# A mixer kernel with other homes for the squares and the gates' weights, and with batch 1's scores over the whole TensorE array

## The chip, the cores and the metric

One core of a Trainium2 chip runs the whole program. The metric is device time in microseconds, and the median of several runs is compared. On a core TensorE (PE), VectorE (DVE), ScalarE (ACT), GpSimd (POOL) and SyncE (SP) each work through a queue of their own; SP here issues nearly all of the transfers between memory (HBM) and SBUF.

## The reference

```python
def _attn_ref(q, k, v):            # B, H, S, D = 2, 8, 768, 64
    k_sum = k.reshape(B, H, nb, 32, D).max(axis=3)      # nb = 24 blocks
    v_sum = v.reshape(B, H, nb, 32, D).mean(axis=3)
    scores_l = scale * q @ k.T                          # kept where |i - j| < 16
    scores_s = scale * q @ k_sum.T + log(32)
    a = softmax(concat(masked scores_l, scores_s))
    return a @ concat(v, v_sum)

def _moe_ref(x, mu_k, mu_r, w_k, w_v, w_r):   # x: B, S, 512; w_k 512x1024
    x_prev = x shifted by one position
    xk = mu_k * x + (1 - mu_k) * x_prev
    xr = mu_r * x + (1 - mu_r) * x_prev
    k = maximum(xk @ w_k, 0)
    return sigmoid(xr @ w_r) * ((k * k) @ w_v)

def _moe2_ref(x, w_tok1, w_tok2, w_ch1, w_ch2):
    h = maximum(x.T @ w_tok1, 0) @ w_tok2     # over the 768 positions
    u = x + h.T
    return u + maximum(u @ w_ch1, 0) @ w_ch2  # 512 -> 1536 -> 512

reference = _moe2_ref(_moe_ref(_attn_ref(q, k, v)))
```

The weights arrive as float64, everything else as float32.

## The kernel before, in words

*Attention.* A tile is 128 positions of one batch. For each tile `s_stage` forms the scores of its 8 heads against 24 block keys and 96 neighbouring keys (120 columns, in `kw`), `t_stage` transposes the exponentials, and `v_stage` multiplies them with the values (`pv`). A head has 64 dimensions, and each half of a tile (64 positions) has its own window of keys, so a score is a 64x120 product of 64-deep operands, and four of them stand in the four quarters of the 128x128 array: two heads (parity `e` = 0, 1 on the two halves of the partitions) by two halves of the tile. One bank of PSUM, tag "s", holds the scores of one parity, four heads by both halves. Batch 0 takes one parity per step, batch 1 both, 16 score matmuls per tile in a fixed line (`in_line`). pv is 64x64 with a depth of 120 and uses half of the array. These products are plain float32, and each shows as two records in the trace.

*Everything else* multiplies in three products of a high and a low part (`mm3`, lines 539 to 546, names `xh`/`xl`, `kh`/`kl`, `gh`/`gl`, and pairs of `w`), each one record on PE. A float64 weight is loaded as words, turned into a float32 by ACT (L153) and DVE (L157, L163), and split by ACT (L174) and POOL (L175).

*The MoE stage* goes in chunks of 256 positions. ko = xk·w_k in 256-column matmuls; `k2_tile` squares the result and splits it into `kh`, `kl`; acc = squares·w_v in 512-column matmuls, the square standing in the array and w_v moving (`values`); ro = xr·w_r the same way (`gate_pass`). Behind it come the token MLP (h and ho) and the channel MLP (go or m, then o at L983 and L955).

*Order.* The program emits attention and the MoE stage side by side by a credit of costs (`attention` and `main`), and a list scheduler with priorities (`ahead`) then fixes the order of each engine's queue. From batch 1 on, scores, transposes and pv stand among ko and acc on PE.

*Where things lie.* [...] Pools grow from the left (const, `ybuf`, stage, work, xp, later w2) and from the right (`r1` with the 16 slots of w_k and w_v, `at` for attention, later `r2` with 12 slots). Before the change `kh` and `kl` lie in work, at 70.7 to 78.7 KB, while w_v lies in r1 at 160 to 224 KB; w_r lies in the first four slots of r2, at 112 to 128 KB, while xr's parts lie at 50.7 to 58.7 KB. `ybuf` at 0.75 to 24.75 KB holds the outputs of the MoE stage for all twelve tiles; in the attention stage part of it serves as room for values.

Of the kernel before, what the change touches and what calls it, by code (L numbers as in the profile page):

```python
# [9 lines left out]
F32 = mybir.dt.float32  # L10
F32R = mybir.dt.float32r
# [16 lines left out]
MW = 256  # L28
# [8 lines left out]
GB = 4  # L37
PIN3, PIN4 = 3, 3
PINL = True
QB = 3  # L40
RSPLIT = 1
HM = 300
VDMA, VEARLY = (1,), 1
# [11 lines left out]


@with_exitstack
def fused_kernel(ctx, tc, q, k, v, vt, mu, w_k, w_v, w_r, w_t1, w_t2, w_c1, w_c2, out):
    nc = tc.nc
    B, NT = q.shape[:2]  # L60
    S, DM = v.shape[1] - WINDOW * 2, v.shape[2]
    H, D = 8, 64
    DFF = w_v.shape[0]
# [158 lines left out]
    def in_line(inst):  # L222

        behind(inst, line[-1:])
        line.append(inst)
# [7 lines left out]
    def after(inst):  # L233

        behind(inst, mark[-1:])
# [8 lines left out]
    for f in range(NF):  # L244
        for i, (src, use) in enumerate(((w_k[f], wk.append),
                                        (w_v[f * 128:(f + 1) * 128, :], wv.append))):
            weights.add(wa if 2 * f + i < NRA else wb, src, use)

    work = pool("work", "left")
    xp = pool("xp", "left", reuse_waits="tile")  # L250
    XB = S + 1
# [95 lines left out]
    @ahead(HL)  # L347
    def q_load(b, t):
        if b == 0:
            st_of(b)["qT"][t] = xT[:, :, XB + 1 + 128 * t:XB + 129 + 128 * t]  # L350
        else:
            st_of(b)["qT"][t] = at.tile([128, NP, 128], F32, tag="qT", bufs=QB, name="qT")
        after(nc.sync.dma_start(st_of(b)["qT"][t], q[b, t]))

    @ahead(HS)
    def s_stage(b, t, es):
        st = state[b]
        mask = masks[1 if t == 0 else 2 if t == NT - 1 else 0]
        kw, qT = st["kw"][t], st["qT"][t]
        sps = [bank("s", 2, [128, NP, NC], "sp") for _ in es]  # L360
        line.clear()
        for p in range(NP):
            for half in range(2):
                c0 = half * (WC - NC)
                for sp, e in zip(sps[::-1], es[::-1]):
                    r = slice(64 * e, 64 * e + 64)
                    m = nc.tensor.matmul(sp[64 * half:64 * half + 64, p], qT[r, p, 64 * half:64 * half + 64],  # L367
                                         kw[r, p, c0:c0 + NC], start=True, stop=True)
                    if len(es) > 1:
                        in_line(m)  # L370
        if PINL:
            mark.append(m)
        zs = []
        for sp, e in zip(sps, es):
            mn = at.tile([128, NP], F32, tag="mn", bufs=4, name="mn")
            if b not in LATE:
                den = at.tile([128, NP], F32, tag="den", bufs=4, name="den")
            else:
                if e == 0:
                    st["den"][t] = at.tile([128, 2, NP], F32, tag="dens", bufs=3, name="dens")  # L380
                den = st["den"][t][:, e]
            P = []
            for p in range(NP):
                pe = at.tile([128, NC], F32, tag="pe", bufs=PEB, name="pe")
                low = nc.vector.tensor_tensor_reduce(out=pe, in0=sp[:, p], in1=mask, op0=ALU.add, op1=ALU.min,  # L385
                                                     scale=-1.0 / math.sqrt(D), scalar=3.0e38, accum_out=mn[:, p:p + 1])
                nc.scalar.activation(pe, pe, AF.Exp, bias=mn[:, p:p + 1], scale=-1.0, accum_out=den[:, p:p + 1])  # L387
                P.append(pe)
            lows.append(low)
            zs.append({"u": (b, t, e), "P": P, "den": den})  # L390
        return zs
# [20 lines left out]
    @ahead(HV)  # L412
    def v_stage(zs):
        b, t, _ = zs[0]["u"]
        st = state[b]
        if t not in st["pv"]:
            st["pv"][t] = bank("pv", 1, [128, NP, 128], "pv")
        pv = st["pv"][t]
        line.clear()
        for p in range(NP):  # L420
            for half in range(2):
                for z in zs[::-1]:
                    e = z["u"][2]
                    h = 2 * p + e
                    m = nc.tensor.matmul(pv[64 * e:64 * e + 64, p, 64 * half:64 * half + 64],  # L425
                                         st["vw"][t][half][0][:, h * D:(h + 1) * D],
                                         z["PT"][:, p, 64 * half:64 * half + 64], start=True, stop=True)
                    if len(zs) > 1:
                        in_line(m)
        if zs[-1]["u"][2] == 1:  # L430
            c0 = b * XB + 1 + 128 * t
            if b not in LATE:
                nc.scalar.copy(xT[:, :, c0:c0 + 128], pv)
            else:
                den = st["den"].pop(t)
                nc.vector.tensor_scalar(den, den, 1e-9, None, ALU.add)
                nc.vector.reciprocal(den, den)
                rb = bank("pt", 2, [128, NP, 128], "rb")
                for p in range(NP):
                    for e in range(2):  # L440
                        nc.tensor.matmul(rb[64 * e:64 * e + 64, p], den[:, e, p:p + 1].to_broadcast([128, D]), ident,
                                         start=True, stop=True)
                x = xT[:, :, c0:c0 + 128]
                nc.scalar.copy(x, pv)
                nc.vector.tensor_tensor(x, x, rb, ALU.mult)
# [64 lines left out]
            q_load(b, 1)  # L510

    def prep(b):

        for t in range(NT):
            k_max(b, t)
            yield HOLD / (NT + 2)
        for j in range(2):
            vt_sum(b, j)
            yield HOLD / (NT + 2)
        kw_sums(b, 0)  # L520
        v_gather(b)
# [29 lines left out]
    @ahead(HM)  # L551
    def k2_tile(o):
        rl = work.tile([128, 2 * MW], F32, tag="rl", bufs=2, name="rl")
        hi = work.tile([128, 2 * MW], F32R, tag="kh", bufs=2, name="kh")
        lo = work.tile([128, 2 * MW], F32R, tag="kl", bufs=2, name="kl")
        nc.scalar.activation(rl, o, AF.Relu)  # L556
        nc.vector.tensor_tensor(rl, rl, rl, ALU.mult)  # L557
        nc.scalar.copy(hi, rl)  # L558
        nc.gpsimd.tensor_tensor(lo, rl, hi.bitcast(F32), ALU.subtract)  # L559
        return hi, lo  # L560
# [81 lines left out]
            q_load(0, t + 1)  # L642
    while weights.todo:
        weights.load()
    masks = []
    for kind in range(3):
        mc = at.tile([128, NC], F32, name=f"mask{kind}")
        mm = work.tile([128, 2, 128], F32, tag="t32", bufs=2, name="mm")
        for half in range(2):
            m = mm[:, half, :NC]  # L650
            nc.gpsimd.memset(m, 0.0)
            first = 64 * half - PAD
            keys = m[:, NB:NC] if half == 0 else m[:, 0:NK]
            for base, cm, st in ((first + EDGE, -1, 1), (EDGE - first, 1, -1)):
                nc.gpsimd.affine_select(out=keys, in_=keys, pattern=[[st, NK]], compare_op=ALU.is_ge, fill=-8.0 * BIG,
                                        base=base, channel_multiplier=cm)
            if kind == 1 and half == 0:
                nc.gpsimd.memset(m[:, NB:NB + PAD], -8.0 * BIG)
            if kind == 2 and half == 1:
                nc.gpsimd.memset(m[:, NK - PAD:NK], -8.0 * BIG)  # L660
            nc.gpsimd.memset(m[:, 0:NB] if half == 0 else m[:, NK:NC], math.sqrt(D) * math.log(BLOCK))
            nc.gpsimd.tensor_scalar(mc[64 * half:64 * half + 64], m[64 * half:64 * half + 64], 1.0, 1.0, ALU.mult, ALU.mult)
        masks.append(mc)
    for t in range(NT):
        ahead(HK)(k_max)(0, t)
    kw_sums(0, 0)
    for z in range(B):
        nc.gpsimd.memset(xT[:, :, z * XB:z * XB + 1], 0.0)
    nc.gpsimd.tensor_scalar(oms, mus, -1.0, 1.0, ALU.mult, ALU.add)
# [20 lines left out]
    R2 = Ring(r2, "w", 12)  # L690
    wr, t1, t2 = [], [], []
    NM = DTOK // 128
    for d in range(KD):
        weights.add(R2, w_r[d * 128:(d + 1) * 128, :], wr.append)
    per = 512 // DTOK
    for i in range(0, NT, per):
        weights.add(R2, w_t1[i * 128:(i + per) * 128, :].rearrange("(a p) n -> p a n", p=128),
# [127 lines left out]
    xp.release()  # L825
    work.release()
    w2 = pool("w2", "left", reuse_waits="tile")
    W2 = Ring(w2, "w", 8)
    CR = Ring(w2, "w", 0)
    CR.slots = R2.slots[:10] + spare + wb.slots + R2.slots[10:]  # L830
    c2_add(0, 0)
    c2_add(0, 1)
    plain_add(2, CR)
# [248 lines left out]
    for got in cd():  # L1082
# [4 lines left out]
                weights.step()  # L1087
    w2.release()
    r2.release()
    r1.release()  # L1090
    stage.release()
    ypool.release()
    const.release()


_INS = ['q', 'k', 'v', 'vt', 'mu', 'moe_w_k', 'moe_w_v', 'moe_w_r',
        'moe2_w_tok1', 'moe2_w_tok2', 'moe2_w_ch1', 'moe2_w_ch2']


def laid_out(q, k, v, mu_k, mu_r, w_k):  # L1100
# [6 lines left out]
    def by_values(x):  # L1107
# [2 lines left out]
    pad = ((0, 0), (0, 0), (WINDOW, WINDOW), (0, 0))  # L1110
    kp = by_values(np.pad(k, pad))
    dm, dff = w_k.shape
    return {
        "q": by_values(q).reshape(B, 2 * D, H // 2, nt, 128).transpose(0, 3, 1, 2, 4),
        "k": np.stack([kp[..., 128 * t:128 * t + 128 + 2 * WINDOW] for t in range(nt)], axis=1),
        "v": np.pad(v, pad).transpose(0, 2, 1, 3).reshape(B, S + 2 * WINDOW, H * D),
        "vt": by_values(v).reshape(B, 2 * D, 2, H // 4 * S).transpose(0, 2, 1, 3),
# [25 lines left out]
```

## Time and profile before

| | |
|---|---|
| median of 3 runs | 503.41 us (502.32 to 503.72) |
| span of the profiled execution | 502.8 us |
| PE busy | 487.9 us, 97% of the span |
| PE's weight loads busy | 407.1 us, 81% |
| DVE, ACT, POOL busy | 316.6, 250.9, 217.4 us |
| granted TensorE clock, mean | 0.990 |

The profile shows no time of the execution beside its span; the median of the runs stands 0.6 us above it. Busy is the union of an engine's instructions, and ends of matmuls are modelled, so the pace of PE is read from one start to the next. A score or pv has two records. [...]

### The profile page before, as it was taken

The numbers are of one execution on the slowest core, as the hardware profiler recorded it, in microseconds if no ns is written. First come the engines' busy times: TensorE is split into PE (matmuls) and PEld (weight loads), VectorE is DVE, ScalarE is ACT, GpSimd is POOL, SyncE is SP. The second block draws the span as 40 slices with busy tenths as digits, with TensorE's granted clock in tenths as the row PEclk, the third lists the DMA queues.
The fourth block names the chain that finished last, engine by engine and source line by source line (L and its number), as shares of the span: only waits on it lengthen the run. The fifth ranks groups of instructions, "written<-read, shape, count | busy, mean of one in ns | idle before, by whom it ended". The sixth has DMA issues, their size and how long they took to land.

```text
span 502.8 us, 8800 instructions
## 1 busy us (share of the span) xinstructions
PE 487.9 (97%) x3278; PEld 407.1 (81%) x3278; DVE 316.6 (63%) x638; ACT 250.9 (50%) x569; POOL 217.4 (43%) x266
## 2 busy tenths in 40 slices
PE   7999997999999999999999998999999999999996
PEld 3567785888888888888888887878898999989995
DVE  2888998641514355598889789646579638354352
ACT  1778746862544555686585455454554435111110
POOL 6335587862441447345516434774942813000000
PEclk9899998899999999999999999999999999999999
DMA  8999930221000650000551998639351405253102
GB/s 264 323 309 361 335 87 14 88 80 40 20 1 2 224 196 0 1 0 14 161 163 21 400 394 313 211 112 316 117 168 42 142 31 164 52 200 117 52 1 83
DMA packets 35914, 70.63 MB, mean 140 GB/s; under 512 B 3072, under 2 KB 12288, under 8 KB 35872
## 3 DMA queue, kind: packets, MB, share of 16 engines
q1 hardware_dynamic: 34288, 69.09, 42.0%
q10 hardware_dynamic: 1584, 0.98, 0.7%
q8 instruction: 26, 0.43, 0.3%
q14 instruction: 16, 0.13, 0.1%
HBM read 60.04 MB, written 9.44 MB: 138 GB/s over the span
## 4 chain that ended last, share of the span: by engine, by line
PE 75%; DMA 10%; DVE 8%; POOL 2%; ACT 2%; issue 1%; SPq 1%; DVEq 0%; POOLq 0%
PE ko L544 13%; PE acc L544 13%; PE o L955 12%; PE m L544 11%; PE o L983 7%; PE ro L544 7%; PE go L544 5%; DMA wst<-in_moe_w_k_dram 3%; DMA xT<-in_q_dram 3%; DMA ybuf<-in_v_dram 2%; DVE wf L163 2%; PE pv L425 2%; PE sp L367 2%; PE h L544 2%; DMA wst<-in_moe_w_ch_dram 1%
## 5 line engine op out<-in xcount | busy, mean ns | idle before, releaser
L175 POOL TENSOR_TENSOR w<-wf,w 128x512 fp32r<-128x512 f32 x50 | 69.1, 1387 | 77.3 <-ACT w L174 72.4
L544 PE MATMUL ko<-xh,w 128*128 128x256 f32 x384 | 76.3, 288 | 1.7 <-POOL w L175 0.9
L544 PE MATMUL m<-u,w 128*128 128x256 f32 x504 | 65.1, 283 | 0.8 <-DVE mw L846 0.7
L544 PEld LDWEIGHTS m<-u,w 128*128 128x128 f32 x504 | 63.4, 191 | 2.9 <-DVE mw L846 0.9
L544 PEld LDWEIGHTS ko<-xh,w 128*128 128x128 f32 x384 | 61.1, 188 | 5.4 <-POOL w L175 1.1
L544 PE MATMUL acc<-w,kh 128*128 128x512 f32 x192 | 61.7, 404 | 0.0
L955 PE MATMUL o<-w,gh 128*128 128x512 f32 x192 | 59.1, 391 | 0.0
L544 PE MATMUL ko<-xl,w 128*128 128x256 f32 x192 | 54.4, 283 | 1.1 <-DVE xl L536 1.1
L559 POOL TENSOR_TENSOR kl<-rl,kh 128x512 fp32r<-128x512 f32 x24 | 33.7, 1405 | 44.6 <-ACT kh L558 36.4
L163 DVE SCALAR_TENSOR_TENSOR wf<-wst,wf 128x512 int32<-128x512 int32 x50 | 47.6, 956 | 8.2 <-ACT wst L153 7.1
L174 ACT CAST w<-wf 128x512 fp32r<-128x512 f32 x50 | 30.9, 620 | 42.8 <-DVE wf L163 40.9
L557 DVE TENSOR_TENSOR rl<-rl 128x512 f32<-128x512 f32 x24 | 19.6, 819 | 48.4 <-ACT rl L556 48.2
L387 ACT ACTIVATE pe<-pe,mn 128x120 f32<-128x120 f32 x96 | 36.6, 383 | 14.6 <-DVE mn L385 14.3
L153 ACT ACTIVATE wst<-wst 128x512 f32<-128x512 f32 x62 | 41.1, 675 | 2.1 <-DMA wst<-in_moe_w_ch_dram 2.1
L544 PEld LDWEIGHTS acc<-w,kh 128*128 128x128 f32 x192 | 35.3, 192 | 7.3 <-ACT pe L387 0.3
L955 PEld LDWEIGHTS o<-w,gh 128*128 128x128 f32 x192 | 34.7, 188 | 6.2
L534 DVE SCALAR_TENSOR_TENSOR xk<-xT,mus,tmp 128x256 f32<-128x256 f32 x52 | 36.5, 733 | 4.1 <-POOL tmp L533 3.2
L544 PEld LDWEIGHTS ko<-xl,w 128*128 128x128 f32 x192 | 36.2, 188 | 2.1 <-DVE xl L536 1.3
L544 PE MATMUL acc<-w,kl 128*128 128x512 f32 x96 | 37.7, 403 | 0.0
L955 PE MATMUL o<-w,gl 128*128 128x512 f32 x96 | 37.1, 391 | 0.0
L544 PE MATMUL go<-u,w 128*128 128x512 f32 x144 | 35.6, 393 | 0.0
L784 ACT ACTIVATE gh<-m 128x512 fp32r<-128x512 f32 x24 | 14.2, 596 | 42.7 <-DVE m L846 42.7
(120 smaller groups left out, 964.5 us busy)
## 6 DMA issues: line engine op xcount, KB each, us to landing
wst<-in_moe_w_ch_dram SPq DMA_DIRECT2D x36, 512.0 KB, 6.9
w<-stored SPq DMA_DIRECT2D x24, 512.0 KB, 4.9
stored<-w SPq DMA_DIRECT2D x24, 256.0 KB, 4.7
wst<-in_moe_w_k_dram SPq DMA_DIRECT2D x8, 512.0 KB, 7.4
wst<-in_moe_w_v_dram SPq DMA_DIRECT2D x8, 512.0 KB, 9.5
wst<-in_moe_w_tok_dram SPq DMA_DIRECT2D x6, 512.0 KB, 4.7
out_dram<-o SPq DMA_DIRECT2D x12, 256.0 KB, 2.4
kw<-in_k_dram SPq DMA_DIRECT2D x9, 320.0 KB, 5.1
```

Source lines behind the costliest of these rows:

```text
L153: a = nc.scalar.activation(top.bitcast(F32), top.bitcast(F32), AF.Prelu, scale=2.0 ** -112, alpha=2.0 ** 32)
L163: nc.vector.scalar_tensor_tensor(wi, top, 3, wi, ALU.logical_shift_left, ALU.bitwise_or)
L174: r = nc.scalar.copy(hi, src)
L175: eng.tensor_tensor(lo, src, hi.bitcast(F32), ALU.subtract)
L387: nc.scalar.activation(pe, pe, AF.Exp, bias=mn[:, p:p + 1], scale=-1.0, accum_out=den[:, p:p + 1])
L534: nc.vector.scalar_tensor_tensor(xk[:, d], xT[:, d, x0:x0 + MW], mu[:, d:d + 1], tmp, ALU.mult, ALU.add)
L544: nc.tensor.matmul(o, l, r, start=(first and i == 0), stop=(last and i == 3 * n - 1))
L557: nc.vector.tensor_tensor(rl, rl, rl, ALU.mult)
L559: nc.gpsimd.tensor_tensor(lo, rl, hi.bitcast(F32), ALU.subtract)
L784: nc.scalar.activation(hi, o, AF.Relu)
L955: nc.tensor.matmul(accs[c][t], l, r, start=(first and j == 0 and i == 0), stop=(last and j == 1 and i == 2))
L983: nc.tensor.matmul(accs[0][t], l, r, start=(k == 0 and i == 0), stop=(k == NF2 - 1 and i == 2))
```

## The change

Three things are edited. First, `kh` and `kl` move from the pool work to a pool `sq` on the right (152 to 160 KB), and w_r moves from r2's slots to a pool `wrp` on the left (28.8 to 44.8 KB), whose four slots later serve as half of the ring `W2`; r2 then lies at 104 to 152 KB and the order of the slots in the ring `CR` changes. Second, batch 1's scores are 8 matmuls of 128x120 per tile: the host lays out q as `qd` with a block of zeros for each head pair, so that a stationary tile of 128x128 holds one half's 64 positions for e = 0 and for e = 1, and a bank now holds one half of the tile for both parities (before: one parity for both halves). The masks for that (`both`) are put together by eight copies on POOL, softmax and v_stage index accordingly, and v_stage issues as many matmuls of the same shape as before. Third, the q tiles of batch 1 are twice as large (512 KB); that of tile 0 has a buffer of its own, and those of tiles 1 to 5 lie in slots of `ybuf` (QHOME). To make room the program's scratch for DMA descriptors shrinks.

```diff
-QB = 3
+QHOME = 8, 10, 6, 8, 10
...
+    sq = pool("sq", "right")
+    wrp = pool("wrp", "left")
...
-            st_of(b)["qT"][t] = at.tile([128, NP, 128], F32, tag="qT", bufs=QB, name="qT")
-        after(nc.sync.dma_start(st_of(b)["qT"][t], q[b, t]))
+            home = slot2(QHOME[t - 1]) if t else at.tile([128, 2 * DM], F32, name="qT")
+            st_of(b)["qT"][t] = home.rearrange("p (g h c) -> p g h c", g=NP, h=2)
+            after(nc.sync.dma_start(st_of(b)["qT"][t], qd[b - 1, t]))
...
-        line.clear()
-        for p in range(NP):
-            for half in range(2):
+        if len(es) == 1:
+            mask = [masks[1 if t == 0 else 2 if t == NT - 1 else 0]]
+            r = slice(64 * es[0], 64 * es[0] + 64)
+            for p in range(NP):
+                for half in range(2):
+                    c0 = half * (WC - NC)
+                    m = nc.tensor.matmul(sps[0][64 * half:64 * half + 64, p], qT[r, p, 64 * half:64 * half + 64],
+                                         kw[r, p, c0:c0 + NC], start=True, stop=True)
+        else:
+
+            mask = [both[:, 1 if t == 0 else 0], both[:, 3 if t == NT - 1 else 2]]
+            line.clear()
+            for half, sp in enumerate(sps):
                 c0 = half * (WC - NC)
-                for sp, e in zip(sps[::-1], es[::-1]):
-                    r = slice(64 * e, 64 * e + 64)
-                    m = nc.tensor.matmul(sp[64 * half:64 * half + 64, p], qT[r, p, 64 * half:64 * half + 64],
-                                         kw[r, p, c0:c0 + NC], start=True, stop=True)
-                    if len(es) > 1:
-                        in_line(m)
+                for p in range(NP):
+                    m = nc.tensor.matmul(sp[:, p], qT[:, p, half], kw[:, p, c0:c0 + NC], start=True, stop=True)
+                    in_line(m)
...
-                for z in zs[::-1]:
-                    e = z["u"][2]
+                for e in (1, 0) if len(zs) > 1 else (zs[0]["u"][2],):
                     h = 2 * p + e
+                    z, c = (zs[half], e) if len(zs) > 1 else (zs[0], half)
                     m = nc.tensor.matmul(pv[64 * e:64 * e + 64, p, 64 * half:64 * half + 64],
                                          st["vw"][t][half][0][:, h * D:(h + 1) * D],
-                                         z["PT"][:, p, 64 * half:64 * half + 64], start=True, stop=True)
+                                         z["PT"][:, p, 64 * c:64 * c + 64], start=True, stop=True)
...
-        hi = work.tile([128, 2 * MW], F32R, tag="kh", bufs=2, name="kh")
-        lo = work.tile([128, 2 * MW], F32R, tag="kl", bufs=2, name="kl")
+        hi = sq.tile([128, 2 * MW], F32R, tag="kh", bufs=2, name="kh")
+        lo = sq.tile([128, 2 * MW], F32R, tag="kl", bufs=2, name="kl")
...
+    both = at.tile([128, 4, NC], F32, name="both")
+    for i, (kind, half) in enumerate(((0, 0), (1, 0), (0, 1), (2, 1))):
+        for e in range(2):
+            rows.append((both[64 * e:64 * e + 64, i], masks[kind][64 * half:64 * half + 64]))
...
+    for dst, src in rows:
+        nc.gpsimd.tensor_copy(dst, src)
...
+    WR = Ring(wrp, "wr", KD)
     for d in range(KD):
-        weights.add(R2, w_r[d * 128:(d + 1) * 128, :], wr.append)
+        weights.add(WR, w_r[d * 128:(d + 1) * 128, :], wr.append)
...
-    W2 = Ring(w2, "w", 8)
+    W2 = Ring(w2, "w", 8 - KD)
+    W2.slots += WR.slots
     CR = Ring(w2, "w", 0)
-    CR.slots = R2.slots[:10] + spare + wb.slots + R2.slots[10:]
+    CR.slots = R2.slots[6:10] + R2.slots[:6] + spare + wb.slots + R2.slots[10:]
```

The change also moves instructions in the queues. In the rows that follow a name such as `acc<-w,kh` is the output and its operands, the shape is that of the output, and xN counts neighbours of one form; the line numbers of after are some ten higher.

First place, PE, where batch 1's tile 3 multiplies with its values. Before, all 16 stand in one block among ko:

```order
L544 MATMUL ko<-xh,w 128x256
L425 MATMUL pv<-PT,vw 64x64 x16
L544 MATMUL ko<-xh,w 128x256
L544 MATMUL ko<-xl,w 128x256
L544 MATMUL ko<-xh,w 128x256
L544 MATMUL acc<-w,kh 128x512 x2
L544 MATMUL acc<-w,kl 128x512
L544 MATMUL acc<-w,kh 128x512 x2
L544 MATMUL acc<-w,kl 128x512
```

Afterwards, two of the 16 come earlier, and the other 14 stand one by one:

```order
L435 MATMUL pv<-PT,vw 64x64
L553 MATMUL ko<-xh,w 128x256
L553 MATMUL acc<-w,kh 128x512
L435 MATMUL pv<-PT,vw 64x64
L553 MATMUL acc<-w,kh 128x512
L435 MATMUL pv<-PT,vw 64x64
L553 MATMUL acc<-w,kl 128x512
L435 MATMUL pv<-PT,vw 64x64
L553 MATMUL acc<-w,kh 128x512
L435 MATMUL pv<-PT,vw 64x64
L553 MATMUL acc<-w,kh 128x512
```

What moved: pv of this tile went from one place between ko to 14 places between ko and acc, mostly after every single acc.

Second place, PE, the scores of batch 1's tiles 0 and 1. Before, they are 64x120 matmuls, 14 and 1 of tile 0 with four acc between, then batch 0's last pv with its reciprocal sums (rb):

```order
L544 MATMUL ko<-xh,w 128x256
L367 MATMUL sp<-kw,qT 64x120 x14
L544 MATMUL acc<-w,kh 128x512 x4
L367 MATMUL sp<-kw,qT 64x120
L425 MATMUL pv<-PT,ybuf 64x64 x8
L441 MATMUL rb<-ident,dens 64x128 x8
L544 MATMUL ko<-xh,w 128x256
```

Afterwards tile 0's 8 stand together, and tile 1's first four come six rows of acc behind the last row shown:

```order
L379 MATMUL sp<-kw,qT 128x120 x8
L553 MATMUL acc<-w,kh 128x512 x4
L553 MATMUL ko<-xh,w 128x256
L553 MATMUL ko<-xl,w 128x256
L320 MATMUL vp<-ident,vrs 24x128 x2
L435 MATMUL pv<-PT,ybuf 64x64 x8
L451 MATMUL rb<-ident,dens 64x128 x8
```

What moved: the odd 64x120 score between acc and batch 0's last pv is gone, two ko and the sums of the values' blocks (vp) stand in its place, and tile 1's scores begin earlier among acc and ko.

Third place, DVE, as batch 1 begins. Before, the conversion of the last weights of the MoE stage (L157 and L163) and the input mix (xk) stand in front of the first softmax row of tile 0 (L385):

```order
L445 TENSOR_TENSOR xT<-xT,rb 128x4x128
L157 TENSOR_SCALAR wf<-wst 128x512
L534 SCALAR_TENSOR_TENSOR xk<-xT,mus,tmp 128x256
L163 SCALAR_TENSOR_TENSOR wf<-wst,wf 128x512
L534 SCALAR_TENSOR_TENSOR xk<-xT,mus,tmp 128x256
L557 TENSOR_TENSOR rl<-rl 128x512
L157 TENSOR_SCALAR wf<-wst 128x512
L385 ISA pe,mn<-sp,mask_182 128x120
```

Afterwards all eight softmax rows of tile 0 stand in front of these (the last one is the first row here, L395), and the first rows of tile 1 (the last row here) come soon behind:

```order
L395 ISA pe,mn<-sp,both 128x120
L395 ISA mn 128x1
L157 TENSOR_SCALAR wf<-wst 128x512
L455 TENSOR_TENSOR xT<-xT,rb 128x4x128
L163 SCALAR_TENSOR_TENSOR wf<-wst,wf 128x512
L157 TENSOR_SCALAR wf<-wst 128x512
L543 SCALAR_TENSOR_TENSOR xk<-xT,mus,tmp 128x256
L406 TENSOR_SCALAR den<-den 128x4
L163 SCALAR_TENSOR_TENSOR wf<-wst,wf 128x512
L543 SCALAR_TENSOR_TENSOR xk<-xT,mus,tmp 128x256
L395 ISA pe,mn<-sp,both 128x120
```

What moved: the softmaxes of tile 0 went ahead of the last conversions and of the mix.

## Rows read from the trace of the kernel before

**Rows 1.** the page's head: the span, and each engine's busy time and instructions.

```profile
span 502.8 us, 8800 instructions
...
PE 487.9 (97%) x3278; PEld 407.1 (81%) x3278; DVE 316.6 (63%) x638; ACT 250.9 (50%) x569; POOL 217.4 (43%) x266
```

**Rows 2.** Two stretches: us, PE busy (xrecords), granted clock, DMA share, GB/s.

```profile
92.00:300.00 208.00, 207.94 (x1418) 1.00 0.30 102
380.00:496.00 116.00, 116.00 (x724) 1.00 0.26 82
```

**Rows 3.** PE's timeline: start us, us, work, xrecords, [idle before <-releaser].

```profile
80.32 0.39 PE L544 MATMUL ko<-xh,w 128*128 128x256 f32 x1 [0.74 <-ACT rl L556]
...
81.75 0.50 PE L544 MATMUL ko<-xh,w 128*128 128x256 f32 x2 [0.93 <-POOL w L175]
...
84.71 0.63 PE L367 MATMUL sp<-kw,qT 64*64 64x120 f32 x2 [1.52 <-issue]
...
307.48 1.89 PE L983 MATMUL o<-w,gh 128*128 128x512 f32 x7 [1.29 <-ACT gh L784]
```

**Rows 4.** PE's timeline, single pv pieces between ko of batch 1's tile 2.

```profile
114.46 1.04 PE L425 MATMUL pv<-PT,vw 120*64 120x64 f32 x28
115.43 0.38 PE L544 MATMUL ko<-xh,w 128*128 128x256 f32 x1
115.74 0.33 PE L425 MATMUL pv<-PT,vw 120*64 120x64 f32 x2
...
116.58 0.50 PE L544 MATMUL ko<-xh,w 128*128 128x256 f32 x2
```

**Rows 5.** the chain that ended last: start us, us, what, xrecords.

```profile
127.34 2.80 PE acc L544 x12
...
151.72 2.84 PE ko L544 x24
...
211.97 4.43 PE ro L544 x19
...
313.26 2.75 PE o L983 x12
```

**Rows 6.** PE's timeline, a block of pv between acc.

```profile
148.89 0.39 PE L544 MATMUL acc<-w,kh 128*128 128x512 f32 x1
149.21 1.15 PE L425 MATMUL pv<-PT,vw 120*64 120x64 f32 x32
150.29 0.50 PE L544 MATMUL acc<-w,kh 128*128 128x512 f32 x1
150.62 0.39 PE L544 MATMUL acc<-w,kl 128*128 128x512 f32 x1
```

**Rows 7.** PE's timeline, two pieces of scores and the ko behind each.

```profile
93.05 1.04 PE L367 MATMUL sp<-kw,qT 64*64 64x120 f32 x30
94.03 0.51 PE L544 MATMUL ko<-xh,w 128*128 128x256 f32 x2
...
130.07 0.64 PE L367 MATMUL sp<-kw,qT 64*64 64x120 f32 x14
130.64 0.39 PE L544 MATMUL ko<-xh,w 128*128 128x256 f32 x1
```

**Rows 8.** PE's groups by shape: xrecords | busy us, mean ns | idle before.

```profile
L544 PE MATMUL acc<-w,kh 128*128 128x512 f32 x192 | 61.7, 404 | 0.0
...
L367 PE MATMUL sp<-kw,qT 64*64 64x120 f32 x192 | 11.7, 299 | 1.6 <-issue 1.5
```

**Rows 9.** PE in two stretches of the start, columns as in rows 2.

```profile
84.00:90.00 6.00, 5.29 (x38) 0.50 0.23 60
90.00:91.00 1.00, 1.00 (x4) 0.62 0.93 291
```

**Rows 10.** POOL's groups by shape: xinstructions | busy us, mean ns | idle before.

```profile
L662 POOL TENSOR_SCALAR mask<-mm 64x120 f32<-64x120 f32 x6 | 1.7, 286 | 0.3
```

**Rows 11.** DMA issues: queue, xcount, KB each, median us to landing.

```profile
qT<-in_q_dram SPq DMA_DIRECT2D x6, 256.0 KB, 3.2
```

More of the change, by code (lines that the diff above doesn't have):

```diff
@@ L57, in fused_kernel @@
 @with_exitstack
-def fused_kernel(ctx, tc, q, k, v, vt, mu, w_k, w_v, w_r, w_t1, w_t2, w_c1, w_c2, out):
+def fused_kernel(ctx, tc, q, qd, k, v, vt, mu, w_k, w_v, w_r, w_t1, w_t2, w_c1, w_c2, out):
     nc = tc.nc
-    B, NT = q.shape[:2]
+    B, NT = k.shape[:2]
     S, DM = v.shape[1] - WINDOW * 2, v.shape[2]
@@ L350, in q_load @@
             st_of(b)["qT"][t] = xT[:, :, XB + 1 + 128 * t:XB + 129 + 128 * t]
+            after(nc.sync.dma_start(st_of(b)["qT"][t], q[t]))
         else:
-            st_of(b)["qT"][t] = at.tile([128, NP, 128], F32, tag="qT", bufs=QB, name="qT")
-        after(nc.sync.dma_start(st_of(b)["qT"][t], q[b, t]))
+            home = slot2(QHOME[t - 1]) if t else at.tile([128, 2 * DM], F32, name="qT")
+            st_of(b)["qT"][t] = home.rearrange("p (g h c) -> p g h c", g=NP, h=2)
+            after(nc.sync.dma_start(st_of(b)["qT"][t], qd[b - 1, t]))
     @ahead(HS)
@@ L357, in s_stage @@
         st = state[b]
-        mask = masks[1 if t == 0 else 2 if t == NT - 1 else 0]
         kw, qT = st["kw"][t], st["qT"][t]
         sps = [bank("s", 2, [128, NP, NC], "sp") for _ in es]
-        line.clear()
-        for p in range(NP):
-            for half in range(2):
-                c0 = half * (WC - NC)
-                for sp, e in zip(sps[::-1], es[::-1]):
-                    r = slice(64 * e, 64 * e + 64)
-                    m = nc.tensor.matmul(sp[64 * half:64 * half + 64, p], qT[r, p, 64 * half:64 * half + 64],
-                                         kw[r, p, c0:c0 + NC], start=True, stop=True)
-                    if len(es) > 1:
-                        in_line(m)
+        if len(es) == 1:
[10 more added lines that the diff above has]
+            for half, sp in enumerate(sps):
+                c0 = half * (WC - NC)
+                for p in range(NP):
+                    m = nc.tensor.matmul(sp[:, p], qT[:, p, half], kw[:, p, c0:c0 + NC], start=True, stop=True)
+                    in_line(m)
         if PINL:
@@ L373, in s_stage @@
         zs = []
-        for sp, e in zip(sps, es):
+        for sp, e, mk in zip(sps, es, mask):
             mn = at.tile([128, NP], F32, tag="mn", bufs=4, name="mn")
@@ L384, in s_stage @@
                 pe = at.tile([128, NC], F32, tag="pe", bufs=PEB, name="pe")
-                low = nc.vector.tensor_tensor_reduce(out=pe, in0=sp[:, p], in1=mask, op0=ALU.add, op1=ALU.min,
+                low = nc.vector.tensor_tensor_reduce(out=pe, in0=sp[:, p], in1=mk, op0=ALU.add, op1=ALU.min,
                                                      scale=-1.0 / math.sqrt(D), scalar=3.0e38, accum_out=mn[:, p:p + 1])
@@ L644, in fused_kernel @@
         weights.load()
-    masks = []
+    masks, rows = [], []
     for kind in range(3):
@@ L1089, in fused_kernel @@
     r2.release()
+    sq.release()
     r1.release()
+    wrp.release()
     stage.release()
@@ L1093, in fused_kernel @@
     const.release()
-_INS = ['q', 'k', 'v', 'vt', 'mu', 'moe_w_k', 'moe_w_v', 'moe_w_r',
+_INS = ['q', 'qd', 'k', 'v', 'vt', 'mu', 'moe_w_k', 'moe_w_v', 'moe_w_r',
         'moe2_w_tok1', 'moe2_w_tok2', 'moe2_w_ch1', 'moe2_w_ch2']
@@ L1112, in laid_out @@
     dm, dff = w_k.shape
+    qt = by_values(q).reshape(B, 2 * D, H // 2, nt, 128).transpose(0, 3, 1, 2, 4)
+    qd = np.zeros((B - 1, nt, 2, D, H // 2, 2, 2, 64), q.dtype)
+    for e in range(2):
+        qd[:, :, e, :, :, :, e] = qt[1:, :, e * D:e * D + D].reshape(B - 1, nt, D, H // 2, 2, 64)
     return {
-        "q": by_values(q).reshape(B, 2 * D, H // 2, nt, 128).transpose(0, 3, 1, 2, 4),
+        "q": qt[0], "qd": qd.reshape(B - 1, nt, 2 * D, H // 2, 2, 128),
         "k": np.stack([kp[..., 128 * t:128 * t + 128 + 2 * WINDOW] for t in range(nt)], axis=1),
@@ L1126 @@
     from concourse.bass_utils import run_bass_kernel_spmd
-    nc = bacc.Bacc("TRN2", target_bir_lowering=False, num_devices=1)
+    nc = bacc.Bacc("TRN2", target_bir_lowering=False, num_devices=1, dynamic_dma_scratch_size=64)
     b, h, s, d = inputs['q'].shape
```

## The prediction

> **What bounds the kernel now.** The first view is the page's head: PE is busy 487.9 us of a span of 502.8 us, DVE, the next, 316.6 [rows 1]. The second is the table by stretches: from 92 to 300 us PE is busy 207.94 of 208 us, and from 380 to 496 us all of 116, both at a granted clock of 1.00 [rows 2]. So from 92 us on, what is added to or taken from PE's queue moves the end by its full length, and what DVE, ACT, POOL and the transfers do costs only where PE then waits. Two places have idle time of any size: 79 to 92 us, and 306 us [rows 3]. The median of the runs, 503.4, lies 0.6 above this execution's span; I sum against 502.8 and add the 0.6 at the end.
>
> Within the full stretches I read three prices from the timeline.
>
> *An excursion.* The scores (64x120 here) and the products with the values, pv (64x64), use only quarters or halves of the array; everything else uses the whole of it. Two single pv between ko matmuls: from 115.43 to 116.58 there are two ko records and two pv of two records each [rows 4]. A ko record in a steady run is 2.84/24 = 0.118 [rows 5]. A pv streams in (1.08 − 0.97)/2 = 0.055: 16 of them take 1.08 to the next start [rows 6], 14 take 0.97, from 114.46 on [rows 4]. So (1.15 − 2×0.118 − 2×0.055)/2 = 0.40 per excursion. A block of 16 among acc: 148.89 to 150.62 is 1.73, less two acc of 0.233, less 16×0.055, is 0.38 [rows 6]. One excursion costs 0.38 to 0.40 however many matmuls it holds, on either neighbour.
>
> *A score.* 15 matmuls (30 records) take 0.98 to the next ko, 7 (14 records) 0.57 [rows 7], so one more costs 0.41/8 = 0.051. Four quadrants work side by side, two records each, so one record of 120 columns occupies its quadrant for about 4×0.051/2 = 0.102.
>
> *A crossing pair.* [...] Where the stationary and the moving operand lie on the two sides of the middle of SBUF the pace of a 512-column record is 2.80/12 = 0.233 (acc) and 4.43/19 = 0.233 (ro); where they lie on one side it is 2.75/12 = 0.229 (o of L983) [rows 5]. That is the inference behind the halves; it is small, 0.004 to 0.0055 a record.
>
> **The change part by part.**
>
> *Excursions.* Read off the order of PE from batch 1's first score on, before has 25 excursions: 18 pieces of scores and 8 of pv, two of them in one. After has no excursion for scores, which are whole-array matmuls there, but pv is torn: 2 + 14 matmuls for tiles 0, 1, 4 and 5, eight pieces for tile 2, and 2 + 14 singles for tile 3, each single between two acc or ko (the first order piece). That is 31, and one with batch 0's last pv: 32. Seven more at 0.395 is **+2.8**. Bounds: 0.38 and 0.40 give 2.7 and 2.8; if a single among acc costs only what it streams, see the rivals.
>
> *Scores.* Before, 96 matmuls stream in 96×0.051 = 4.9. After, 8 whole-array matmuls per tile, 2 records each, 96 records in all (half of the 192 shown in [rows 8]). No row shows one. From below, the same 120 columns in a quadrant take 0.102; from above, a ko record, which also brings its own 128-column weights, takes 0.118 [rows 5]. That is 9.8 to 11.3; I take the middle, 0.110, so 10.6: **+5.7** (4.9 to 6.4). Half of the array does nothing useful in them, since half of q's tile is zeros.
>
> *Halves.* acc has 192 kh records [rows 8] and, by the three products of each pair, half as many kl, ro 12 tiles × 4 × 3 = 144: 288 + 144 = 432 records, now crossing, which the new pools put on one side each. 432×0.005 = **−2.2**, bounds 0 (these families differ in more than the place) and −2.5. The 256-column ko and m show no such difference, so nothing is taken for them.
>
> [...]
>
> *The early stretch.* Before loses, from 79 to 92 us, idle time of 0.74, 0.93 and 1.52 [rows 3] (with the ends of the modelled matmuls some 0.8, 1.1, 1.6 and 0.2, together 3.7), and then a clock of 0.50, the lower of the two levels, from 84 to 90, and a mean of 0.62 to 91 [rows 9]: 5.29 busy us at half speed and one at 0.62 do 2.6 + 0.4 = 3.0 us less work than at 1.00. Together 6.7. In the new order the softmaxes of batch 1's tile 0 stand ahead of the last weights' conversions on DVE (the third order piece), and the scores of tiles 1 and 2 and their transposes come earlier on PE (the second). Each whole-tile step now needs two banks freed by softmaxes of all eight heads: going through the new order by hand with the durations of before, I find PE idle for about 4.5 (scores of tile 2 behind the softmax 1.7, transposes behind POOL's division 1.0, and three smaller ones), spread differently, with a clock loss of anything between 0 and 3. I take **−1.0**; bounds −6.7 (all of it gone) and +2 (waits of 6 and the clock loss kept).
>
> *The stall at 306 us.* o of L983 waits 1.29 for ACT's gh there [rows 3], behind a chain of loads and conversions that starts only when the last ro has freed slots for the weights of the channel MLP. In the new queue on SP four of these loads (the third quarter of w_ch1's plain part) stand ahead of the others instead of behind them, since w_r no longer holds slots of that ring. Some of the chain is conversions, which keep their number: **−0.5**, bounds −1.3 and 0.
>
> *Nothing taken for:* the eight masks copied by POOL, 8×0.286 = 2.3 by the row of the same shape [rows 10]; they lie in the first 50 us, where the first loads are waited for, and if POOL were the last there they would cost 2.3. The doubled q tiles, 6×256 KB more: a 256 KB tile lands in 3.2 us [rows 11], 512 KB perhaps in 5 to 7, under a stretch in which PE has 80 us of work and the DMA engines are below a third busy; late q tiles would stop PE at once, by up to 3 each, but each is asked for more than a tile ahead. The smaller DMA scratch and the changed column arithmetic in v_stage add no instruction.
>
> *Sum:* +2.8 + 5.7 − 2.2 − 1.0 − 0.5 = +4.8: span 502.8 → 507.6, median **508.2 us**.
>
> **The rivals.** 0.3% of 503 us, 1.5 us, is about what a measurement of this kernel can tell from no change.
>
> *A, the sum as it stands:* 508.2, its own range 505.5 to 510.5 (scores ±0.8, the early stretch −2 to +2, the halves' last half).
>
> *D, the halves move nothing:* acc and ro keep 0.233, because the 0.004 comes from something else in these stages, as their eviction or what runs on DVE beside them. 508.2 + 2.2 = 510.4. For it: the difference is 2% of a record; against it: both crossing families agree to three digits.
>
> *C, the early stretch closes:* the new order removes the three waits and with them the drop of the clock, −6.7 instead of −1.0, so 502.5: no change. For it: the 1.52 wait that precedes the drop has no releaser that the profile shows (it stands as issue, before a score), and scores as one piece of the whole-array queue do away with the excursion there. Against it: the same softmaxes, transposes and weights are to be done between batch 0 and batch 1. It decides as soon as the clock stays at 1.00 through 80 to 95 us and the idle time there is under 0.5.
>
> *B, single pv pieces cost only what they stream:* TensorE may take a pv of 64x64 between two acc without emptying, since an acc of 512 columns gives it 0.23 to load in, twice what a ko gives. The blocks of 14 and 16 would keep their price; of the 23 single or small pieces among acc and ko each saves 0.39, −9.0: 499.2, faster. Against it: in [rows 4] two singles among ko cost 0.40 each, and the block among acc [rows 6] no less than one among ko.
>
> **How the numbers follow.** A 0.56, D 0.12, C 0.17, B 0.15. Faster by over 0.3% (B) 0.15; within 0.3% (C) 0.17; slower (A, D) 0.68. The range that leaves out B alone reaches from C, less 1.0 for the stall and the cheaper scores, to D, plus 1.1 for the upper price of a score and a longer early wait: 501.5 to 511.5. As cases of both signs hold some chance, A's own range stands above.
>
> **What the profile of the changed kernel will show.** Right, if: the 128x120 records follow each other at 0.102 to 0.118; each single pv between two acc of tile 3 takes 0.43 to 0.46 from its start to the second next acc less 0.233, 14 times; 512-column acc and ro records come at 0.228 to 0.229; idle time and clock loss between 79 and 95 us together are 4 to 7 us; and the wait at the first o of L983 is shorter than 1.29. From the start of batch 1's first scores to the last values PE must have some 7 us more work. Wrong, if singles ride at 0.06; if the score records run in pairs well under 0.1, as the 0.051 of quadrants; if the clock stays full in the early stretch; or if a q tile or a bank comes late and PE shows a new wait inside 100 to 180 us.

## The result and the profile after

The changed kernel takes 510.08 us (median of 4 runs, 509.75 to 512.7) where the kernel before takes 503.26 (4 runs): ratio 1.0127, 95% interval 1.0089 to 1.0165. It is slower, as forecast, 1.9 us above the forecast 508.2 and inside the range of 501.5 to 511.5. The profiled execution has a span of 508.2 us at a time of 510.03. Some executions of the kernel before fall into a slower state (509 to 511 us); its medians in the experiments leave these out.

The page's head, which answers to [rows 1], and PE's two stretches as in [rows 2] with the low-clock stretch of [rows 9]:

```profile
span 508.2 us, 8635 instructions
...
PE 493.4 (97%) x3182; PEld 414.5 (82%) x3182; DVE 320.0 (63%) x638; ACT 250.8 (49%) x569; POOL 218.1 (43%) x274
```

```profile
83.00:90.00 7.00, 6.78 (x31) 0.52 0.24 99
92.00:300.00 208.00, 207.18 (x1302) 1.00 0.30 98
386.00:500.00 114.00, 114.00 (x715) 1.00 0.27 84
```

PE has 96 records fewer and is busy 5.5 us longer; the span is 5.4 longer. The bound has not changed, and the clock still falls for seven microseconds in the early stretch. The clock is given as a share of full speed, and the records of both traces hold 1.00 and 0.50 alone: by half microseconds it is 0.50 from 84.0 to 90.5 us before and from 83.5 to 90.0 after, with 0.93 or 0.75 only in the windows at the edges. At 0.50 a ko record takes 2.57/12 = 0.214 (the chain of after, from 86.74 us on), at 1.00 it takes 0.1167 (below).

PE's timeline of after (start, duration, work, records) answers to [rows 4] and [rows 6]: tile 3's single pv between single acc. From one pv to the next is 0.69 us; less an acc of 0.229 and a pv of 0.055, each piece costs 0.40.

```profile
124.68 0.33 PE L435 MATMUL pv<-PT,vw 120*64 120x64 f32 x2
124.94 0.50 PE L553 MATMUL acc<-w,kh 128*128 128x512 f32 x1
125.37 0.33 PE L435 MATMUL pv<-PT,vw 120*64 120x64 f32 x2
125.63 0.51 PE L553 MATMUL acc<-w,kl 128*128 128x512 f32 x1
126.07 0.33 PE L435 MATMUL pv<-PT,vw 120*64 120x64 f32 x2
```

The same timeline for whole-array scores, beside [rows 7]. From 77.51 to 79.57 lie eight score records and ten ko; with ko at its pace of 0.1167 (below), a score record takes (2.06 − 1.17)/8 = 0.112. The 0.81 from the first score to the first ko would give 0.101, but that is too little: the first ko behind such a group takes 0.2 to the next, not 0.117 (two take 0.32 from 78.32 to 78.64), and these 0.085 belong to the scores. Inside a group the starts are 0.111 to 0.112 apart.

```profile
77.51 1.05 PE L379 MATMUL sp<-kw,ybuf 128*128 128x120 f32 x8
78.32 0.48 PE L553 MATMUL ko<-xh,w 128*128 128x256 f32 x2
78.64 0.28 PE L553 MATMUL ko<-xl,w 128*128 128x256 f32 x1
...
79.57 1.05 PE L379 MATMUL sp<-kw,ybuf 128*128 128x120 f32 x8
```

The groups by shape (busy us, mean ns, idle before, releaser), where batch 1's pv of the same 192 records is, first before, then after (with most of its scores in the last line):

```profile
L425 PE MATMUL pv<-PT,vw 120*64 120x64 f32 x192 | 7.5, 226 | 0.0
```

```profile
L435 PE MATMUL pv<-PT,vw 120*64 120x64 f32 x192 | 13.4, 233 | 0.0
L379 PE MATMUL sp<-kw,ybuf 128*128 128x120 f32 x80 | 12.9, 301 | 2.0 <-DVE mn L395 1.9
```

The records have hardly grown (226 to 233 ns): what fills the 5.9 us more is the edge of each piece, where no other pv overlaps it.

The chain that ended last, answering to [rows 5]: acc at 2.75/12 = 0.229, ro at 4.32/19 = 0.2274, ko at 2.80/24 = 0.1167.

```profile
175.07 2.75 PE acc L553 x12
177.81 2.80 PE ko L553 x24
...
217.22 4.32 PE ro L553 x19
```

And the waits of PE, answering to [rows 3]: the longest early one is now tile 2's scores behind the softmax of tile 1; the stall at the first o of L1000 has gone from 1.29 to 0.89; and one before ro is new.

```profile
82.52 1.43 PE L379 MATMUL sp<-kw,ybuf 128*128 128x120 f32 x8 [1.90 <-DVE mn L395]
...
275.52 0.73 PE L553 MATMUL ro<-w,xh 128*128 128x512 f32 x2 [0.68 <-DVE ybuf L731]
...
313.31 2.14 PE L1000 MATMUL o<-w,gh 128*128 128x512 f32 x8 [0.89 <-ACT gh L800]
```

### The profile page after: what moved, and what is told of

Same layout as the page of the kernel before. It is cut to its first block, busy times and chain, and to the rows that moved or that the text cites. A ratio compares the mean times of both kernels' runs of the same rounds, so it can differ in the third digit from the quotient of the medians.

```text
span 508.2 us, 8635 instructions
## 1 busy us (share of the span) xinstructions
PE 493.4 (97%) x3182; PEld 414.5 (82%) x3182; DVE 320.0 (63%) x638; ACT 250.8 (49%) x569; POOL 218.1 (43%) x274
## 4 chain that ended last, share of the span: by engine, by line
PE 72%; DMA 10%; DVE 10%; issue 4%; POOL 3%; ACT 1%; SPq 0%; POOLq 0%; DVEq 0%
PE ko L553 13%; PE o L972 12%; PE acc L553 12%; PE m L553 11%; PE o L1000 6%; PE go L553 5%; DMA ybuf<-in_v_dram 4%; PE ro L553 4%; PE pv L435 3%; DMA wst<-in_moe_w_ch_dram 2%; POOL w L175 2%; DMA wst<-in_moe_w_k_dram 2%; DVE wf L163 2%; PE sp L379 2%; PE pt L415 1%
## 5 line engine op out<-in xcount | busy, mean ns | idle before, releaser
L163 DVE SCALAR_TENSOR_TENSOR wf<-wst,wf 128x512 int32<-128x512 int32 x50 | 48.3, 971 | 4.5 <-ACT wst L153 3.3
L543 DVE SCALAR_TENSOR_TENSOR xk<-xT,mus,tmp 128x256 f32<-128x256 f32 x52 | 37.6, 754 | 1.9 <-POOL tmp L542 1.0
```

The lines of the kernel that those rows point to most:

```text
L163: nc.vector.scalar_tensor_tensor(wi, top, 3, wi, ALU.logical_shift_left, ALU.bitwise_or)
L543: nc.vector.scalar_tensor_tensor(xk[:, d], xT[:, d, x0:x0 + MW], mu[:, d:d + 1], tmp, ALU.mult, ALU.add)
```

## The experiments

The theory: each excursion from whole-array matmuls to smaller ones costs about 0.39 us on PE, and the torn pv (31 pieces in batch 1) gives back more than the scores' excursions saved; the scores' streams add some 5 us; the new places of squares and w_r give 1 to 2. The rivals: the small pieces are free and something else cost the time; the places do nothing; PE waits elsewhere.

**The places alone.** The kernel before with `sq`, `wrp`, the slots and the smaller DMA scratch; scores and their order as before.

```diff
-        hi = work.tile([128, 2 * MW], F32R, tag="kh", bufs=2, name="kh")
-        lo = work.tile([128, 2 * MW], F32R, tag="kl", bufs=2, name="kl")
+        hi = sq.tile([128, 2 * MW], F32R, tag="kh", bufs=2, name="kh")
+        lo = sq.tile([128, 2 * MW], F32R, tag="kl", bufs=2, name="kl")
...
-        weights.add(R2, w_r[d * 128:(d + 1) * 128, :], wr.append)
+        weights.add(WR, w_r[d * 128:(d + 1) * 128, :], wr.append)
```

> The kernel before with the places alone changed: squares in the upper half, w_r in the lower, the ring's slots and the smaller DMA scratch with them; scores as before. Theory (a crossing pair paces 512-column records at 0.233 instead of 0.229): acc falls to 0.229 and ro to 0.228, 288 x 0.004 + 144 x 0.005 = 1.9 us less, and the stall at 306 us shrinks by some 0.4: span about 500.5, ratio to before about 0.995. Rival (the place moves nothing): acc and ro stay at 0.233, ratio 1.000 and at most the 0.4 of the stall. If the time outside the span grows by 1.2 us as it did in the changed kernel, the scratch or the pools cause it and not the larger q.

Measured: 502.90 us (12 runs) against 503.71 (22 runs), ratio 0.9996 (0.9967 to 1.0024): one of the twelve took 509.45. The interval holds the rival's 1.000 and leaves out the theory's 0.995. The trace shows what moved. The chain of this kernel:

```profile
164.31 2.75 PE acc L546 x12
...
208.68 4.32 PE ro L546 x19
```

acc runs at 0.229 and ro at 0.2274, so the pace follows the new places, and the rival's 0.233 falls. But not all of it comes: the time between the starts of acc and ro records, less 0.229 for each (at full clock, with whole-array work on both sides), sums to 1.09 for acc and 0.82 for ro in the kernel with the small scratch alone (below), and to 0.48 and 0.41 here. That is 1.0 us, not 1.9 to 2.2: runs of twelve acc lie between 0.2275 and 0.2325 here, and a shorter run of ro at 0.230. And part of it is given back: in front of ro PE now waits for DVE, by 0.94 at 267.31 us here and 0.68 in the changed kernel (at 275.52, shown above). This wait is 0.64 to 0.95 in all seven kernels with the new places, 0.21 in the two with the old places and the small scratch, and absent in the three with the large scratch.

What it is about the places is open. The two sides of 112 KB, the middle of the 224 KB over which the program's pools stretch, do not explain it, by a row of the chain of the changed kernel:

```profile
289.50 2.49 PE h L553 x11
```

Its r2 begins at 104 KB. Seven of these eleven h have their stationary operand there, below 112 KB, and all have the moving one at 160 KB or above; they cross the middle and run at 2.49/11 = 0.226. And some acc are no faster for lying on one side: squares at 152 KB with the part of w_v at 164 KB follow each other at 0.232 to 0.234 in the changed kernel and in this one. Another property divides the two groups as well: in these programs the pools from the left start at a multiple of 64 bytes and those from the right 32 bytes past one; acc and ro of the old places join one kind with the other, and acc and ro of the new places, h and the o of L983 do not. No run separates this from the sides.

**The DMA scratch alone.**

```diff
-    nc = bacc.Bacc("TRN2", target_bir_lowering=False, num_devices=1)
+    nc = bacc.Bacc("TRN2", target_bir_lowering=False, num_devices=1, dynamic_dma_scratch_size=64)
```

> The kernel before with the smaller DMA scratch alone. Theory: nothing, ratio 1.000 within 0.3%. Rival: the time outside the span, 1.8 us in the changed kernel, comes from the scratch, then the time rises by about 1.2 us (ratio 1.002) at the same span.

Measured: 503.56 (12 runs), ratio 0.9996 (0.9980 to 1.0012). The time outside the span is 1.8 us here (504.58 at a span of 502.8), and so in every run of every kernel that names both: the rival falls. One thing moved that I had put at nothing: ko. Its chain, with acc as before:

```profile
150.14 2.80 PE ko L544 x24
152.94 2.80 PE acc L544 x12
```

2.80 instead of the 2.84 of [rows 5], as in all kernels with the small scratch and in none with the large one. 576 ko records × 0.0016 are 0.9 us in the trace; the median moved by 0.2, within its spread.

**The scores alone.** The changed kernel with squares and w_r back in their old places (the first diff the other way round); the small scratch stays.

> The changed kernel with squares and w_r back in their old places: whole-array scores, the same torn pv pieces as after. Theory: acc and ro go back to 0.233, so 1.9 to 2.5 us above the changed kernel, span about 510.5, ratio to before 1.015 to 1.019. Rival (places move nothing): span 508.2, ratio 1.0127 like the changed kernel.

Measured: 510.81 us (6 runs), ratio 1.0134 (1.0108 to 1.0161), below the theory's 1.015 and next to 1.0127 for the whole change: the time does not tell the two apart. The chain shows acc back at 2.80 for 12 (for example at 163.14). So the places are worth 1.1 us by the rows and some 0.7 by the medians, which is within the spread, and the slower time is the scores' part of the change alone.

**pv in whole blocks.** The changed kernel with another priority and the later half first, so that the first pv is the one that is ready last.

```diff
-HL, HK, HR, HV, HS, HN, HT = 0, 100, 0, 400, 0, 0, 400
+HL, HK, HR, HV, HS, HN, HT = 0, 100, 0, 500, 0, 0, 400
...
-            for half in range(2):
+            for half in (1, 0) if len(zs) > 1 else (0, 1):
```

> The changed kernel with pv kept whole: priority of v_stage 500 instead of 400 and the later half's probabilities first, so each tile of batch 1 has one piece of 16 pv (6 instead of 31 pieces, 8 excursions instead of 32). Theory (0.39 us per excursion): 24 x 0.39 = 9.4 us less, span about 499, ratio to before about 0.993. Rival 1 (small pieces cost only what they stream): same as the changed kernel, ratio 1.0127. Rival 2 (a whole block waits longer for its probabilities): PE shows waits in front of pv that give back 2 to 5 us, span 501 to 504.

Measured: 501.46 us (7 runs), ratio 0.9948 (0.9921 to 0.9974), 8.6 us below the changed kernel. Rival 1 falls. Its timeline has one piece per tile, and its group of batch 1's pv is back below that of before:

```profile
121.07 1.15 PE L435 MATMUL pv<-PT,vw 120*64 120x64 f32 x32
```

```profile
L435 PE MATMUL pv<-PT,vw 120*64 120x64 f32 x192 | 6.9, 225 | 0.0
```

In the stretch from 93 to 180 us the changes of mode (records beside one, start to start, less the steady pace) fall from 11.1 us with 31 pieces to 1.8 with 6: 0.37 each. The priority moves batch 0 too (15 excursions instead of 18 in the first 50 us), and PE waits 1.1 us more there and 1.2 more from 50 to 68 us; that is what is missing from the 9.4.

**Pieces of 2 and 14.** The same priority, the earlier half still first.

> The changed kernel with v_stage's priority at 500, but the earlier half's probabilities still first: every tile of batch 1 has pv pieces of 2 and 14 (14 excursions in batch 1) where the version with whole blocks has 16 (8). Theory (0.39 us per excursion, whatever it holds): 6 x 0.39 = 2.3 us above the version with blocks, span about 501.9, ratio to before about 0.999. Rival (a piece of two matmuls costs only its stream): as the version with blocks, span 499.6, ratio 0.995.

Measured: 502.52 us (10 runs), ratio 0.9984 (0.9955 to 1.0012), 1.1 us above the version with blocks by the medians and 1.8 by the ratios, where the theory has 2.3 and the rival nothing. The modes from 93 to 180 us cost 3.55 where the blocks cost 1.81, for six pieces more: 0.29 each. A piece of two matmuls is not free, and it is somewhat cheaper than 0.39: 0.33 to 0.36 between ko, 0.22 to 0.30 where a transpose stands beside it.

**The kernel before again.**

> The kernel before, unchanged, on the chip of the other runs of this call. Theory: its profiled execution at 502.8 us was long by about 1.2 us against its own median, through a low clock between 12 and 16 us and late first loads; here the clock stays up there and the span is 501.5 to 502.5. ko's pace: 0.118 again if the place of the operands sets it, 0.117 if it belongs to the execution.

Measured: 503.51 us (10 runs), ratio 1.0000 (0.9975 to 1.0026); the profiled execution took 504.6 at a span of 502.8. The expectation fails: the clock is low between 12 and 16 us here too. ko is at 0.118 again, so its pace belongs to the kernel. Three windows (us, PE busy, granted clock, DMA share, GB/s), the first two of this run and the last of the kernel with the small scratch:

```profile
12.20:15.50 3.30, 3.30 (x28) 0.50 1.04 360
84.00:90.00 6.00, 4.94 (x47) 1.00 0.20 45
```

```profile
12.20:15.50 3.30, 3.30 (x43) 1.00 1.04 368
```

Both have the same order on PE. At 51 us the same record starts 1.9 us later here (51.75) than with the small scratch (49.85); 0.9 of that stand ahead of the dip, among the first loads, and 1.0 in it. The spans are equal all the same: the kernel with the small scratch has its clock at 0.54 from 84 to 90 us, and it loses 1.1 us more between 263 and 308 us.

The second window says something of the early stretch. This execution has the same three waits as [rows 3] (0.74, 0.93 and 1.51), and its clock stays at 1.00 behind them, where it was 0.50 in [rows 9]. So the waits alone do not bring the drop. And the full clock gives back 1.0 us by 115 us and not 3.0, because transposes then wait for POOL's division, which stands in this run's chain for 1.05 us from 89.77 us on. What the run also shows is that this profiled execution, and the one that I summed against, are 1.1 us longer than their own kernel's median.

**The priority alone, and on top of the new places.** HV at 500 as above, first on the kernel before, then on the kernel with the new places; scores in quadrants in both, 41 excursions by the order instead of 49.

> The kernel before with v_stage's priority at 500 and nothing else: the same order of PE as the version with the new places and this priority, 41 excursions instead of 49. Theory: 8 x 0.39 = 3.1 us off what priority costs elsewhere, which the version with new places showed as 2.9 by medians (502.9 to 500.0), so about 501, ratio 0.994; acc and ro stay at 0.233 and ko at 0.118, 1.0 and 0.9 us above the version with new places. Rival (the gain needs the new places): ratio 0.998 to 1.000.

> The places changed, scores in quadrants as before, v_stage's priority 500. By the order 41 excursions where the kernel with the places alone has 49. Theory: 8 x 0.39 = 3.1 us less, span about 497.0 to 498, ratio to before about 0.993. Rival: earlier pv waits for probabilities, PE idles before pv and the gain is halved, span 498.5 to 499.5.

Measured: 501.62 us (12 runs), ratio 0.9971 (0.9945 to 0.9997), and 500.02 (8 runs), ratio 0.9932 (0.9907 to 0.9957). Fewer excursions help without the new places, by 1.7 us of 3.1; the ratio lies below the rival's 0.998, but its interval reaches into it. PE's waits between 68 and 93 us rose from 3.8 to 5.5. With the places the time is 1.6 less than without, where the rows of acc, ro and ko would make 1.9; the ratio is the 0.993 expected, and the span, 498.5, stands 0.5 above the theory's 497 to 498, at the edge of the rival.

**Scores and pv side by side.** Priority 500 for scores and pv in both batches, and then for batch 1's scores alone.

```diff
-                zs = s_stage(b, t, es)
+                zs = ahead(500 if b else 0)(s_stage)(b, t, es)
```

> The places changed, scores in quadrants as before, priority 500 for scores and pv, so that most tiles have one piece of scores beside one of pv: 32 excursions by the order where the whole-array version with blocks has 28. Theory: against that version (499.6) the scores stream in 4.7 us less, four excursions and some six changes from scores to pv inside an excursion cost 1.6 + 1.2, so span about 497.7, ratio about 0.991. Rival: scores pulled ahead of everything wait for banks and softmaxes, PE idles 3 to 5 us more between 50 and 180 us, span 500 to 503.

> The version with new places, scores in quadrants and pv at priority 500, with batch 1's scores at priority 500 too: 35 excursions by the order instead of 41, the early part of the order unchanged. Theory: 6 x 0.39 = 2.3 us less than 500.0, less about 0.2 for each of some five changes between scores and pv inside an excursion, so 498.5 to 499, ratio 0.990. Rival: scores taken earlier wait for a bank, PE idles in front of them between 100 and 180 us and nothing is gained, 500 to 501.

Measured: 500.03 us (10 runs), ratio 0.9952 (0.9923 to 0.9981): no better than without, since the early order of batch 0 then makes PE wait more (6.1 us in the first 50, against 4.4) and the clock drops three times (its mean is 0.989, against 0.993 without the scores' priority). With batch 1 alone: 498.23 us (6 runs), ratio 0.9896 (0.9870 to 0.9921), faster than both kernels by more than the uncertainty. Its timeline has scores and pv in one excursion, in whole pieces:

```profile
97.65 0.83 PE L368 MATMUL sp<-kw,qT 64*64 64x120 f32 x18
98.41 1.15 PE L426 MATMUL pv<-PT,vw 120*64 120x64 f32 x32
99.49 0.63 PE L368 MATMUL sp<-kw,qT 64*64 64x120 f32 x12
...
104.20 1.15 PE L426 MATMUL pv<-PT,vw 120*64 120x64 f32 x32
105.28 1.05 PE L368 MATMUL sp<-kw,qT 64*64 64x120 f32 x32
```

## Why the prediction was right, and where its terms were off

I compared the starts of PE's records in both traces; from the first to the last is 5.56 us longer after. The two orders are the same at first and again from 205 us on. Up to 63 us after is 1.5 shorter (loads, and the clock, whose mean from 10 to 17 us is 1.00 after and 0.76 before); from there to 205 us it becomes 6.8 longer. Then it gains 0.5 up to 258 us, loses 1.0 up to the first o of L983, and gains 0.3 behind that. By the terms of the prediction:

- **Scores: +5.8 measured, +5.7 forecast.** A whole-array record takes 0.112, near the middle of the bounds, 0.110: 96 × 0.112 = 10.7, less 4.9. This is the largest term, and it was right.
- **Excursions and the early stretch: +1.7 together, +2.8 − 1.0 = +1.8 forecast.** The price (0.40 for tile 3's singles) and the counts (25 and 32 in the traces) were right; pieces of two pv cost less, 0.30 to 0.35. The two terms can't be parted cleanly, because three excursions of before stand beside its early waits or under its low clock: with 0.4 for each of them the excursions make +1.5 and the early stretch +0.2, with nothing +2.7 and −1.0. The torn pv is what makes the change lose: the block version, with 24 excursions fewer, took back 8.6 us, and with it the same whole-array scores are at 501.5.
- **In the early stretch** the idle time that the timeline shows falls from 3.2 to 2.5 us, and the clock is low for 6.8 us in both (from 83.9 to 90.8 before and from 83.2 to 90.1 after). Rival C fell with it. The wait of tile 2's scores that I had put at 1.7 is 1.90; that of the transposes behind POOL's division, put at 1.0, is some 0.6 (at 84.03 and 84.53 us). The repeated run of before shows that the upper price of this stretch, −6.7 for waits and clock together, was too large: a full clock gave back 1.0 there and not 3.0.
- **Halves: −1.0 measured, −2.2 forecast.** The pace moved as forecast in long runs, 0.233 to 0.229 and 0.2274, so rival D fell; the gain is 1.0 between the kernels with and without the places, 1.1 between after and the scores alone, about half of what 432 records at the full difference make. The faster ro then waits for DVE, 0.68 in front of it and 0.83 with what follows, which the prediction did not have. The mechanism that it named, the two sides of SBUF's middle, was an inference; no run shows it, and it does not fit the row of h (0.226 across the middle). Where only the places differ, the rows show acc at 0.229 and ro at 0.2274 instead of 0.233, 2% less, whatever it is about the places.
- **The stall at 306: −0.4 measured, −0.5 forecast.** But the kernel with the scores alone, whose ring of slots is the old one, has 0.90 as well, so the order of the slots is not shown to be the cause.
- **Nothing was forecast for ko and for the first 63 us; −0.9 and −1.5 measured**, the first with the smaller scratch.

The span was forecast at 507.6 and is 508.2. The mechanism of the two large terms was right; that the sum comes so close is in part luck, since the halves' half and the new wait stand against ko and the first loads, for which nothing was taken.

**The step that failed is the one from span to median.** I added the 0.6 by which the median of before stood above its span. Every run shows 1.8 between span and time (1.74 to 1.91); the profiled execution of before, 502.8 + 1.8 = 504.6, was itself 1.2 above its median, so the 0.6 was a difference of two things. From a typical execution of before (span 501.5) the change costs 6.8, not 5.4. Which part of these 1.2 us is chance is open: the repeated profile was as long.

Rival B, the one on the other side, falls by the rows (0.40 for each single between acc) and by the block version.

## What to carry to other kernels

On a PE that is full, count the pieces of differently tiled matmuls in the order that the scheduler made, at about 0.4 us each in these traces (0.29 for pieces of two), before counting columns; an edit of which matmul comes first, or a priority that keeps a dependent line of small matmuls together (8.6 us for both with pv in blocks), is worth more here than a better use of the array. Making the scores whole-array saved their 18 pieces, some 7 us, and cost 5.8 in columns, so it could win little more than 1, and tore the pv in passing. With pv in blocks the quadrant scores are ahead in spite of 13 excursions more (500.02 against 501.46 us). Before summing against a profiled execution, find its own time beside its span.

## What the runs showed that I had not expected

The pace of a 256-column ko record changed from 2.84/24 to 2.80/24 when nothing but the program's DMA scratch shrank; every kernel with the large scratch shows 0.1183, every one with the small 0.1167. With the small scratch all pools from the left lie 16 KB further left (`ybuf` is at 16.7 to 40.7 KB in the kernel before; 0.75 to 24.75 KB is its place afterwards). The distance is not what counts: xh starts at 34.75 KB with the small scratch alone and at 50.75 KB with the new places, at the same pace, and at 50.69 KB before. The places at 34.75 and 50.75 KB are multiples of 256 bytes and the one at 50.69 KB is not; whether that is the cause was not tried.

A score of 120 columns over the whole array takes 0.112 a record, and one in a quadrant 0.102: in the trace of before four records start within 0.02 us, and the next four 0.102 behind them (from 93.21 us on). The 0.101 that the first row of a group seems to give is a trap: time that a group costs can stand in the interval of the record behind it (the 0.2 of the first ko above, where 0.117 is its pace), so a pace is read inside a long run or over a whole period.
